# Scaling a chunk's sums of exponentials on ScalarE instead of VectorE, in an attention and maxout feed-forward kernel

## The chip, the core and the metric

The kernel runs on one core of a Trainium2 chip. The metric is device time of one execution in microseconds (us). The core has TensorE (PE, with its weight loads PEld), VectorE (DVE), ScalarE (ACT), GpSimd (POOL) and SyncE (SP), which issues DMAs. Each engine has a queue of its own, works it off in order, and waits on semaphores for the others.

## The reference: what is computed

Attention over 8 batches and 12 heads, 448 rows of 64, with normalised queries and keys, and a feed-forward layer with the larger of three products:

```python
q_n, k_n = rmsnorm(q, g_q), rmsnorm(k, g_k)
scores = np.matmul(q_n, k_n.transpose(0, 1, 3, 2)) / np.sqrt(64)
scores = scores - np.max(scores, axis=-1, keepdims=True)
attn = np.exp(scores)
attn = attn / (np.sum(attn, axis=-1, keepdims=True) + 1e-09)
x = np.matmul(attn, v)        # heads side by side: 3584 x 768
h = np.maximum(np.maximum(x @ w1, x @ w2), x @ w3)
out = h @ w_out
```

All tensors are float32. The weights are 768x768.

## The kernel before, in words

**Tiling.** Two heads make a pair; there are 48 pairs, six for each batch. A pair's 448 query rows are cut into four chunks of 112 rows. One chunk's scores, 112 rows by 448 keys for each of the two heads, lie in one PSUM tile `sc`, of which there are two (`bufs=2`). So the scores of chunk k+1 can't be written before chunk k-1 has been read for the last time.

**Two kinds of pairs.** The first six pairs (`PLAIN = 6`) work in float32. From the seventh pair on, each float32 value is split into an upper and a lower float16 part, and a product takes three matmuls. The change touches only this second kind: 42 pairs, 168 chunks.

**One chunk from the seventh pair on.** `scores` (L553) writes `sc` on PE. `row_max` (L562, DVE) takes the negative maximum of each row. `softmax` runs on ACT: L570 scales the maxima into `nm`, and L579 takes the exponentials of each head in place, with the sums of a row accumulated into two spare columns of `sc`; the trace shows each as an ACTIVATE and a short read of the accumulator. `upper_weights` makes the factor of a row: add the epsilon, scale by 2^-15, invert (`rs`, L648 and L652, both DVE). Then ACT multiplies the exponentials by it and keeps the upper half as float16 (`pp`, L655, one for each head). `lower_weights` (L665, DVE) makes the lower half, and with it the last read of `sc`. `turn_weights` transposes `pp` by DMA, and a pair later `add_values` (L703, PE) multiplies by the values.

**What runs beside it.** The next pair's keys and queries are split on ACT (`kp`, `qp`, L434) and POOL (L440), their squares are summed on DVE (L372). The feed-forward layer of the batch before is spread over the chunks: PE does 18 matmuls for each block of the hidden layer (L732), ACT copies the first product (`m`, L742), DVE takes the maxima (L746), ACT and DVE split the result (`ht`, L752 and L756), and the second product leaves through ACT (`osb`, L805). A pair's attention output is split by ACT (`xt`, L717) and DVE (L718). Until about 285 us the weights are still being decoded and split, on DVE and ACT as well.

**What sets the order.** The program is written out by hand. A pair has 12 beats, three to a chunk. In the first beat of a chunk stand its row maximum, its softmax and the lower half of the chunk before; in the second `upper_weights`; in the third the scores of the next chunk. Each beat ends with a share of the feed-forward matmuls and with work that was put off by a number of beats (`later`). What a beat issues lands in the engines' queues in that order, so between an engine's part of `softmax` and of `upper_weights` stands whatever else the first beat gave to it.

Of the kernel before, what the change touches and what calls it, by code (L numbers as in the profile page):

```python
# [12 lines left out]
AF = mybir.ActivationFunctionType  # L13
ALU = mybir.AluOpType
# [4 lines left out]
SUM_EPS = 1e-9  # L19
# [7 lines left out]
P_UP = 2.0 ** 15  # L27
# [12 lines left out]
def qknorm_attention_maxout_ffn_kernel(  # L40
# [35 lines left out]
    nc = tc.nc  # L76
    B, H, S, D = q.shape
# [4 lines left out]
    QP = S // NQ  # L82
# [561 lines left out]
    def upper_weights(g, c):  # L644
        s = st[g]
        sc = s["sc", c]
        rs = sb.tile([QP, 2], F32, name="rs", bufs=3)
        nc.vector.tensor_scalar(  # L648
            out=rs, in0=sc[:QP, 1, S + 8:S + 10], scalar1=SUM_EPS, scalar2=1.0 / P_UP,
            op0=ALU.add, op1=ALU.mult,  # L650
        )
        nc.vector.reciprocal(rs, rs)  # L652
        pp = sb.tile([QP, 2, 2, S], F16, name="pp", bufs=3)
        for h in range(2):
            nc.scalar.activation(  # L655
                pp[:, 0, h], sc[:QP, h, :S], AF.Copy, scale=rs[:, h:h + 1]
            )
        s["pp", c] = pp
        s["rs", c] = rs
# [196 lines left out]
    for i, src in enumerate((g_q, g_k)):  # L856
        nc.scalar.dma_start(
            out=gains[:, i], in_=src.rearrange("(o d) -> o d", o=1).broadcast_to([P, D])
# [61 lines left out]
    def beat(g, i):  # L920
# [15 lines left out]
        if part == 1:  # L936
            if 0 < k <= 4 * PLAIN:
                keep_turned(*divmod(k - 1, 4))
            if PLAIN <= g < G:
                upper_weights(g, c)  # L940
# [123 lines left out]
```

## Time and profile before

| | |
|---|---|
| runs, us | 1097.57, 1104.33, 1100.64 (median 1100.64) |
| the profiled execution | 1099.43 us, span 1097.6 us |
| instructions in the profile | 18387 |
| mean granted PE clock | 0.964 |

The span is the time from the first to the last instruction of the program. A row of the timeline has the start and the length in us, then engine, line, operation, tiles and shapes; behind `x1` may stand the idle time before it and what ended it. A row of the waits has the waiting engine, tile and line, what it waited for, the total in us, the number of waits and the longest. A row of a group has the number of instructions, their busy time in us, the mean of one in ns, then the engine's idle time ahead of them.

### The profile page before, as it was taken

Reading aid. Unit: us, or ns where it says so; the run is one execution under the profiler, and the core shown is the slowest. Engines: PE = TensorE matmul, PEld = TensorE weight load, DVE = VectorE, ACT = ScalarE, POOL = GpSimd, SP = SyncE. Lnnn points to the kernel's source line nnn. Section 1 sums busy time; section 2 is a strip of 40 time slices with the busy share of each in tenths; the row PEclk is TensorE's granted clock in tenths of the full one; section 3 lists DMA queues with packets and bytes.
Section 4 is the critical chain, followed back from the end, with each engine's and each line's share of the span. In section 5 each row is a group of like instructions: output and inputs, shape, how many; then the busy total and the mean of one; then the engine's idle time right before and its main releaser. Section 6 shows DMA issues by size and latency. Waiting matters only on the chain. (4 is left out here: it accounts for less than half of the span.)

```text
span 1097.6 us, 18387 instructions
## 1 busy us (share of the span) xinstructions
PE 1011.4 (92%) x6168; PEld 499.4 (45%) x6168; DVE 755.7 (69%) x1390; ACT 771.8 (70%) x1767; POOL 704.2 (64%) x805
## 2 busy tenths in 40 slices
PE   4678769888899999999999999999999999999998
PEld 2333334334444454444544454444444554445554
DVE  4799988888767676777677767777676766761110
ACT  4598888767878687787877787777777787863101
POOL 5477988866767777677777776777777677610000
PEclk9697869999999999999999999999999999999999
DMA  5554566855887779778887798787877797553002
GB/s 152 164 168 149 131 183 135 192 116 121 164 156 143 145 153 179 152 148 144 168 156 147 138 168 172 148 145 155 174 145 140 140 178 142 108 100 73 1 1 57
DMA packets 426493, 152.28 MB, mean 139 GB/s; under 512 B 372896, under 2 KB 422048, under 8 KB 426400
## 3 DMA queue, kind: packets, MB, share of 16 engines
q1 hardware_dynamic: 425888, 150.95, 67.7%
q8 instruction: 48, 0.79, 0.3%
q14 instruction: 45, 0.37, 0.1%
q10 hardware_dynamic: 512, 0.18, 0.1%
HBM read 51.97 MB, written 11.01 MB: 57 GB/s over the span
## 5 line engine op out<-in xcount | busy, mean ns | idle before, releaser
L732 PE MATMUL acc<-xt,w_sb 128*128 128x448 f16 x2592 | 516.8, 355 | 0.0
L732 PEld LDWEIGHTS <-w_sb 128*128 128x128 f16 x2592 | 244.1, 98 | 259.3 <-issue 47.9
L579 ACT ACTIVATE sc<-sc,nm,down 112x448 f32<-112x448 f32 x336 | 234.2, 697 | 11.2
L562 DVE TENSOR_REDUCE sc<-sc 112x2 f32<-112x896 f32 x192 | 209.6, 1092 | 46.0 <-PE sc L553 44.7
L655 ACT ACTIVATE pp<-sc,rs 112x448 f16<-112x448 f32 x336 | 194.8, 632 | 46.6 <-ACT sc L579 40.9
L665 DVE SCALAR_TENSOR_TENSOR pp<-sc,rs,pp 112x448 f16<-112x448 f32 x336 | 212.9, 675 | 3.4 <-ACT pp L655 2.9
L387 POOL TENSOR_TENSOR ri<-ri,half_neg 128x7 f32<-128x7 f32 x96 | 154.2, 1606 | 8.0
L553 PE MATMUL sc<-kt,qt 64*112 64x448 f16 x1008 | 131.9, 367 | 28.8 <-DVE pp L665 25.0
L570 ACT ACTIVATE nm<-sc,down 112x2 f32<-112x2 f32 x192 | 50.7, 264 | 147.5 <-DVE sc L562 146.1
L796 PE MATMUL acc<-wo_sb,ht 128*128 128x384 f16 x864 | 151.0, 329 | 1.5 <-DVE ht L756 0.8
L761 POOL COPY hx<-ht 128x128 f16<-128x128 f16 x48 | 15.5, 323 | 197.1 <-DVE ht L756 191.1
L796 PEld LDWEIGHTS <-ht 128*128 128x128 f16 x864 | 81.6, 99 | 67.2 <-issue 13.5
L703 PE MATMUL av<-pt,vp 128*64 128x448 f16 x1008 | 108.3, 356 | 0.0
L553 PEld LDWEIGHTS <-qt 64*112 64x112 f16 x1008 | 54.8, 126 | 98.3 <-issue 57.8
L648 DVE TENSOR_SCALAR rs<-sc 112x2 f32<-112x2 f32 x168 | 26.6, 158 | 94.6 <-ACT sc L579 94.6
L440 POOL TENSOR_TENSOR kp<-kn,kp 128x512 f16<-128x512 f32 x42 | 50.0, 1191 | 58.9 <-ACT kp L434 58.9
L703 PEld LDWEIGHTS <-vp 128*64 128x64 f16 x1008 | 49.6, 108 | 55.7 <-issue 30.0
L718 DVE SCALAR_TENSOR_TENSOR xt<-av,xt 128x448 f16<-128x448 f32 x42 | 26.2, 625 | 70.8 <-ACT xt L717 70.8
L372 DVE TENSOR_REDUCE ss<-sq 128x7 f32<-128x448 f32 x96 | 60.9, 635 | 10.6 <-ACT sq L363 6.6
L531 POOL TENSOR_TENSOR vp<-vr,vp 128x448 f16<-128x448 f32 x42 | 43.8, 1044 | 30.3 <-ACT vp L525 30.2
L440 POOL TENSOR_TENSOR qp<-qn,qp 112x512 f16<-112x512 f32 x42 | 49.2, 1173 | 19.8 <-ACT qp L434 19.8
L517 POOL TENSOR_SCALAR vr<-vr,v_up 128x448 f32<-128x448 f32 x42 | 61.1, 1456 | 0.0
(112 smaller groups left out, 1200.4 us busy)
## 6 DMA issues: line engine op xcount, KB each, us to landing
raw<-in_moe_w_dram SPq DMA_DIRECT2D x18, 768.0 KB, 4.5
qr<-in_q_dram SPq DMA_DIRECT2D x48, 224.0 KB, 3.1
vr<-in_v_dram SPq DMA_DIRECT2D x96, 96.0 KB, 2.6
kr<-in_k_dram SPq DMA_DIRECT2D x95, 96.0 KB, 3.1
raw<-in_moe_w_out_dram SPq DMA_DIRECT2D x6, 768.0 KB, 5.0
pt<-pp SPq DMA_TRANSPOSE x168, 4.0
out_dram<-osb SPq DMA_DIRECT2D x8, 336.0 KB, 3.2
out_dram<-osb SPq DMA_DIRECT2D x8, 288.0 KB, 3.6
```

What stands on the lines that cost most here:

```text
L372: nc.vector.tensor_reduce(sums[g % 2][:sq.shape[0], KQ[what]], sq, axis=AX, op=ALU.add)
L387: nc.gpsimd.tensor_tensor(out=ri, in0=ri, in1=half_neg[:, at], op=ALU.pow)
L440: nc.gpsimd.tensor_tensor(out=parts[:, 1], in0=n, in1=parts[:, 0], op=ALU.subtract)
L517: nc.gpsimd.tensor_scalar(out=vr, in0=vr, scalar1=v_up[:, g // NP:g // NP + 1], scalar2=None, op0=ALU.mult,)
L553: nc.tensor.matmul(sc[:QP, h, :S], qt[rows, qp, c], kt[rows, kp, KEYS[h]], start=n == 0, stop=n == len(TERMS) - 1,)
L562: nc.vector.tensor_reduce(sc[:QP, 0, S + 8:S + 10], sc[:QP, :, :S], axis=AX, op=ALU.max, negate=True)
L579: nc.scalar.activation(to, sc[:QP, h, :S], AF.Exp, bias=nm[:, h:h + 1], scale=down[:QP], accum_out=total,)
L655: nc.scalar.activation(pp[:, 0, h], sc[:QP, h, :S], AF.Copy, scale=rs[:, h:h + 1])
L665: nc.vector.scalar_tensor_tensor(out=pp[:, 1, h], in0=sc[:QP, h, :S], scalar=rs[:, h:h + 1], in1=pp[:, 0, h], op0=ALU.mult, op1=ALU.subtract,)
L703: nc.tensor.matmul(av[half, :S], vp[rows, group, vpart], pt[rows, 7 * wp + group], start=u == 0 and n == 0, stop=u == 3 and n == len(TERMS ...
L732: nc.tensor.matmul(acc[:, :S], wt[:, wp, c], xs[c][:, xp], start=(c == 0 and n == 0), stop=(c == NCT - 1 and n == 2),)
L796: nc.tensor.matmul(acc[:, :HW], lhs, wo_sb[:, f, wp, half * HW:(half + 1) * HW], start=(f == 0 and n == 0), stop=(f == NFT - 1 and n == 2),)
```

## The change

In `upper_weights` the epsilon is added and the scaling done by an ACTIVATE (Copy) with constant bias and scale on ScalarE, so sums·2^-15 + epsilon·2^-15; VectorE only inverts.

```diff
         rs = sb.tile([QP, 2], F32, name="rs", bufs=3)
-        nc.vector.tensor_scalar(
-            out=rs, in0=sc[:QP, 1, S + 8:S + 10], scalar1=SUM_EPS, scalar2=1.0 / P_UP,
-            op0=ALU.add, op1=ALU.mult,
+        nc.scalar.activation(
+            rs, sc[:QP, 1, S + 8:S + 10], AF.Copy, bias=SUM_EPS / P_UP, scale=1.0 / P_UP
         )
         nc.vector.reciprocal(rs, rs)
```

All lines behind it move up by one (L655 becomes L654, and so on).

ScalarE's queue in the first chunk of a pair, with the split of the next pair's keys (`kp`) and a copy of the feed-forward layer (`m`) between the exponentials and `pp`; before:

```order
L570 ACTIVATE nm<-sc,down 112x2 [waits DVE_49]
L579 ACTIVATE sc<-sc,nm,down 112x448 [waits Activation_49] x2
L434 CAST kp<-kn_90 128x512 [waits DMAHW2_49]
L742 COPY m<-acc 128x448
L655 ACTIVATE pp<-sc,rs 112x448 [waits DMAHW1_49,DVE_49,Activation_49]
L655 ACTIVATE pp<-sc,rs 112x448
L434 CAST qp<-qn 112x512 [waits DMAHW3_49]
```

and with the change:

```order
L570 ACTIVATE nm<-sc,down 112x2 [waits DVE_49]
L579 ACTIVATE sc<-sc,nm,down 112x448 [waits Activation_49] x2
L434 CAST kp<-kn_90 128x512 [waits DMAHW2_49]
L741 COPY m<-acc 128x448
L648 ACTIVATE rs<-sc 112x2 [waits Activation_49]
L654 ACTIVATE pp<-sc,rs 112x448 [waits DMAHW1_49,DVE_49]
L654 ACTIVATE pp<-sc,rs 112x448
L434 CAST qp<-qn 112x512 [waits DMAHW3_49]
```

The scaling stands behind both pieces and right ahead of `pp`.

VectorE's queue from the lower half of the chunk before to the next row maximum, in the same chunk; before:

```order
L665 SCALAR_TENSOR_TENSOR pp<-sc,rs,pp 112x448
L648 TENSOR_SCALAR rs<-sc 112x2 [waits Activation_49]
L652 RECIPROCAL rs<-rs 112x2 [waits DVE_49]
L372 TENSOR_REDUCE ss_87<-sq 128x7 [waits Pool_49]
L746 TENSOR_TENSOR m<-acc,m 128x448 [waits PE_49,Activation_49]
L562 TENSOR_REDUCE sc<-sc 112x2 [waits PE_49]
```

and with the change:

```order
L664 SCALAR_TENSOR_TENSOR pp<-sc,rs,pp 112x448
L651 RECIPROCAL rs<-rs 112x2 [waits Activation_49]
L372 TENSOR_REDUCE ss_87<-sq 128x7 [waits Pool_49]
L745 TENSOR_TENSOR m<-acc,m 128x448 [waits PE_49]
L562 TENSOR_REDUCE sc<-sc 112x2 [waits DVE_49,PE_49]
```

The reciprocal now waits for ScalarE itself, everything behind it stands as before, and the row maximum names VectorE's own semaphore too.

## The prediction

> **What bounds the kernel now.** I read the page's busy shares first, then busy time by stretches, then the waits of two stretches, then single chunks in the timeline.
>
> ```profile
> PE 1011.4 (92%) x6168; PEld 499.4 (45%) x6168; DVE 755.7 (69%) x1390; ACT 771.8 (70%) x1767; POOL 704.2 (64%) x805
> ```
>
> TensorE (PE) is busy 92% of the span, VectorE (DVE) and ScalarE (ACT) 70%. The chain of work that ended last lies in the last 108 us, where no chunk is left, and tells nothing of the part that is changed. The stretches do:
>
> ```profile
> 145.00:285.00 140.00, 117.53 (x696) 55.97 (x692) 118.98 (x209) 107.93 (x233) 109.16 (x110) 0.94 0.70 145
> 450.00:900.00 450.00, 445.40 (x2829) 217.22 (x2828) 323.49 (x639) 343.88 (x807) 325.43 (x391) 1.00 0.81 154
> ```
>
> The columns are PE, PEld, DVE, ACT, POOL, then clock and DMA. From 145 to 285 us (pairs seven to twelve, while weights are still being decoded) PE idles 22 of 140 us and DVE is busy 85%. From 450 to 900 PE idles only 4.6 of 450 us. Who waits for whom in these two zones, first 140 to 287, then 287 to 992:
>
> ```profile
> PE sc L553 <- DVE pp L665: 18.2, 10, 3.9
> DVE sc L562 <- PE sc L553: 1.7, 2, 1.2
> ...
> DVE sc L562 <- PE sc L553: 43.0, 34, 2.2
> ACT pp L655 <- ACT sc L579: 38.5, 74, 0.7
> ACT pp L655 <- DVE rs L652: 2.1, 3, 0.7
> PE sc L553 <- DVE pp L665: 6.8, 14, 1.3
> ```
>
> In the first zone PE waits for DVE's lower_weights (L665), which frees the score buffer that the next scores (L553) fill: the loop of DVE and ACT is the bound, with 1.7 us of slack in it. In the second zone it is the other way round: DVE waits 43.0 us for scores before its row maximum (L562), and PE waits 6.8 us. That 43.0 us is the loop's whole reserve there.
>
> The loop of one chunk is: row maximum on DVE, nm and two exponentials on ACT, sums and reciprocal on DVE, what DVE has queued, the next row maximum. Three chunks of it, the last row of each exponential first:
>
> ```profile
> 602.51 0.13 ACT L579 ACTIVATION_READ_ACCUMULATOR sc<-sc,nm,down 112x1 f32 x1
> 602.56 0.62 ACT L434 CAST kp<-kn 128x512 f16<-128x512 f32 x1
> 602.87 0.17 DVE L652 RECIPROCAL rs<-rs 112x2 f32<-112x2 f32 x1
> 603.12 1.16 ACT L655 ACTIVATE pp<-sc,rs 112x448 f16<-112x448 f32 x2
> ...
> 613.03 0.13 ACT L579 ACTIVATION_READ_ACCUMULATOR sc<-sc,nm,down 112x1 f32 x1
> 613.20 0.16 DVE L648 TENSOR_SCALAR rs<-sc 112x2 f32<-112x2 f32 x1 [0.73 <-ACT sc L579]
> 613.39 0.17 DVE L652 RECIPROCAL rs<-rs 112x2 f32<-112x2 f32 x1
> 613.64 1.16 ACT L655 ACTIVATE pp<-sc,rs 112x448 f16<-112x448 f32 x2 [0.48 <-ACT sc L579]
> ...
> 617.37 0.13 ACT L579 ACTIVATION_READ_ACCUMULATOR sc<-sc,nm,down 112x1 f32 x1
> 617.78 0.15 DVE L648 TENSOR_SCALAR rs<-sc 112x2 f32<-112x2 f32 x1
> 617.96 0.17 DVE L652 RECIPROCAL rs<-rs 112x2 f32<-112x2 f32 x1
> ...
> 624.10 0.17 DVE L652 RECIPROCAL rs<-rs 112x2 f32<-112x2 f32 x1
> 624.30 0.54 ACT L742 COPY m<-acc 128x448 f32<-128x448 f32 x1
> 624.72 1.18 ACT L655 ACTIVATE pp<-sc,rs 112x448 f16<-112x448 f32 x2
> ```
>
> In a **bare** chunk (613) ACT has nothing between its exponentials and pp and stands still 0.48 us for DVE. In a **covered** chunk (602, 624) ACT does one or two other pieces there, and DVE finishes the reciprocal beside them, at no cost. ACT's waits count the bare ones in the second zone: 74 + 3 = 77 of its 144 chunks; the other 67 are covered.
>
> **The change part by part.** Prices first:
>
> ```profile
> L570 ACT ACTIVATE nm<-sc,down 112x2 f32<-112x2 f32 x192 | 50.7, 264 | 147.5 <-DVE sc L562 146.1
> L619 ACT ACTIVATE sum<-sum 112x8 f32<-112x8 f32 x6 | 1.4, 235 | 0.0
> L652 DVE RECIPROCAL rs<-rs 112x2 f32<-112x2 f32 x168 | 27.9, 166 | 5.8
> L648 DVE TENSOR_SCALAR rs<-sc 112x2 f32<-112x2 f32 x168 | 26.6, 158 | 94.6 <-ACT sc L579 94.6
> L665 DVEq EVENT_SEMAPHORE  x163: 21/50/195, 162.6 to 992.2; - x163
> ```
>
> Removed: 168 DVE operations of 158 ns, 26.6 us of DVE time. Added: 168 ACT operations on the same 112x2 sums. No row has exactly this form. Nearest are nm (264 ns, same shape from PSUM, but the scale read from a tile) and the guard of the first six pairs (235 ns, Copy with constants, 8 elements from SBUF). I take 235, since constants are the nearer form, and keep 264 above; below it I let it be as quick as DVE's 158. That is 39.5 us more ACT time, 811 of 1098 us: as a share, no bound.
>
> In a sentence apart: the Trainium skill (ScalarE: Activation LUTs, What ACT_TABLE_LOAD costs) gives an ACTIVATE with constants 186 ns plus 0.833 ns an element, and 93 ns more for each operand read from a tile, so an estimate of 188 ns here; the trace's 235 for 8 elements is above its 193, and by the page's price the sum below would come out some 7 us lower.
>
> What costs is the place. The new operation stands in ACT's queue behind the covering pieces, right ahead of pp, and the reciprocal must wait for it; hand-overs are read from the rows: 0.04 us from ACT to DVE, 0.08 from DVE's end to pp.
> - Bare: exponential ends 613.16, reciprocal ended 613.56. Now 613.18 + 0.235 + 0.04 + 0.166 = 613.62: +0.06 us.
> - One covering piece: ACT is free at 603.12. Reciprocal ends 603.12 + 0.235 + 0.04 + 0.166 = 603.56 instead of 603.04: +0.52. And pp starts 0.08 later, 603.64 instead of 603.12: ACT too loses 0.52.
> - Two pieces: 624.72 + 0.44 = 625.16 instead of 624.27: +0.89; three are worse.
> - Late DVE (617): DVE comes to the sums 0.28 us after the exponentials' end; the reciprocal can now take the place of the sums' scaling: 0.16 to 0.18 earlier, a gain.
>
> Queued behind the waiting reciprocal on DVE are the sum of squares (L372), the feed-forward's maximum and lower part (L746, L756), the next row maximum and lower_weights, for which PE's scores wait. Behind the waiting pp on ACT are the q cast, ht, m and xt, of which ht and xt hold DVE up in turn. No DMA is moved; the transposes behind pp and kp follow their producers. One more thing in the instruction order: of 192 row maxima 133 now wait for an earlier DVE operation besides PE. That one ended a chunk before, so I price only the extra wait: 0.02 us, between 0 and the median of 0.05 that lower_weights' own separate wait takes (last row above, min/median/max in ns).
>
> Sum, zone one (24 chunks, 7 bare): 10 with one piece, 4 with two, 3 with three, counted in the timeline. The pieces here are longer:
>
> ```profile
> 162.06 0.17 DVE L652 RECIPROCAL rs<-rs 112x2 f32<-112x2 f32 x1
> 163.92 1.15 ACT L655 ACTIVATE pp<-sc,rs 112x448 f16<-112x448 f32 x2
> ```
>
> This reciprocal goes from 162.23 to 163.92 + 0.44 = 164.36, +2.1. Chunk by chunk the 24 give 13 us of delay. Slack is 1.7, so **+11**; at worst 13, at best 0 if DVE's decode fills its new waits.
>
> Sum, zone two: 77 bare, of which some 27 with late DVE, give about −1 together; 50 singly covered at 0.5 give 25; 17 with more at 1.0 give 17. In all 41 us of delay against 43.0 us of reserve. It would just fit, were both spread alike. They are not. Take the twelve pairs from 599.7 to 840, a pattern that recurs:
>
> ```profile
> DVE sc L562 <- PE sc L553: 13.5, 11, 2.2
> ...
> 608.12 0.77 PE L553 MATMUL sc<-kt,qt 64*112 64x448 f16 x6 [1.26 <-DVE pp L665]
> 614.53 1.10 DVE L562 TENSOR_REDUCE sc<-sc 112x2 f32<-112x896 f32 x1 [0.97 <-PE sc L553]
> ...
> 829.73 1.10 DVE L562 TENSOR_REDUCE sc<-sc 112x2 f32<-112x896 f32 x1 [1.48 <-PE sc L553]
> ```
>
> The reserve sits once in a pair, before its last row maximum, and is (first and last of the 11 rows above) 0.97, 0, 2.13, 2.19, 0.98, 0.25, 1.47, 0.69, 1.52, 1.61, 0.25 and 1.48 us. The delays, worked out the same way, are 0.5, 1.54, 2.05, 0.5, 0.95, 1.48, 0.88, 0.95, 2.5, 0.5, 1.93 and 0.88. Where the delay is larger the excess stays: 1.54 + 1.23 + 0.26 + 0.98 + 1.68 = 5.7 us in 240. Over the zone's 705 us that is 17. The extra wait adds about 2. **+19**; at best 0 (the two-deep score buffer carries the excess into the next pair's reserve), at worst 41 (PE's own delay moves the reserve along, so none of it is used).
>
> Together 11 + 19 = 30. The profiled execution took 1099.43 us (span 1097.6), which becomes 1129.4; the median of the runs, 1100.64, lies 1.2 above it, which would make 1130.6. I say **1130**.
>
> **The rivals.**
> - *Reserve fully used.* Zone two costs nothing, zone one 11: 1111 to 1112. For it: delay and reserve are equal in sum. Against it: one pair in four has 0.25 us of reserve or none, and there the delay is about 1.5 or more.
> - *Reserve not used at all.* 13 + 41 = 54: 1155. For it: PE already stands 1.26 us for lower_weights at 608.12, and where it does, any delay of the loop is PE's too. Against it: most pairs show DVE waiting for PE a full microsecond.
> - *Hidden.* DVE's decode in zone one does not depend on the reciprocal and fills the new waits: 1101 to 1105. Against it: each engine's queue is in order, and the decode stands behind the reciprocal.
> - *Faster.* DVE bounds zone one, and gets back 0.19 us (613.20 to 613.39) in each chunk: 24 chunks, 4.6 us; over all 168 chunks 32 us, 1069 at the most. It decides where ACT has the sums scaled before DVE comes to the reciprocal, as in the chunk at 617. Against it: DVE waited 94.6 us for ACT's exponentials before the 168 scalings, so it is ACT that is late there, and ACT gets the work.
>
> **How the numbers follow.** The forecast has 0.68, reserve not used 0.14, reserve used 0.10, hidden 0.04, faster 0.04. A change of 1% is 11 us, about what a measurement of this kernel can tell from no change; between 1090 and 1112 lie the hidden case and parts of the one with the reserve used and of the faster one: 0.10. Slower by more: 0.88; faster by more: 0.02. The range takes in zone one alone (1111) and most of the way to no reserve (1155): 1110 to 1152.
>
> **What would show it.** Right: ACT has 168 operations of about 0.235 us at L648; DVE's waits ahead of the reciprocal grow from 94.6 us to some 160 to 180 (0.28 more in a bare chunk, 0.7 or more in a covered one); DVE's wait for scores in the second zone falls well under 43 us; PE's wait for lower_weights grows there from 6.8 us by some 15; bare chunks pass almost unchanged. Wrong: PE's idle time in 450 to 900 stays at 5 us (then the reserve held), or zone one is no longer than before (then the decode fills the waits), or the reciprocal comes sooner in covered chunks (then the order on ACT isn't what I take it for).

## The result and the profile after

Six runs each: the medians are 1110.53 us with the change (1108.65 to 1111.37) and 1098.34 before (1097.57 to 1104.33). The ratio, taken over all runs and not from the two medians, is 1.0097, 95% interval 1.0078 to 1.0116: about 10.7 us slower. The direction is the forecast one; the size, +30, is nearly three times too large. The profiled execution took 1108.65 us, its span is 1106.9.

The page's busy shares with the change:

```profile
PE 1014.5 (92%) x6168; PEld 497.3 (45%) x6168; DVE 722.1 (65%) x1222; ACT 796.6 (72%) x1935; POOL 705.0 (64%) x805
```

VectorE's busy time fell by 33.6 us, and ScalarE's rose by 24.8. Neither share says anything of the time. The new operation itself (minimum, median and maximum in ns), and the matmuls of the scores, which are as long as before:

```profile
L648 ACT ACTIVATE rs<-sc x168: 152/173/202, 147.1 to 998.9; 112x2 f32<-112x2 f32 x168
L553 PE MATMUL sc<-kt,qt x1008: 346/349/620, 135.9 to 995.5; 64*112 64x448 f16 x168
```

The operation takes 173 ns, not 235. The waits from 290 us on, where before 43.0 us stood for VectorE's wait for scores and 6.8 us for PE's wait for lower_weights:

```profile
DVE rs L651 <- ACT rs L648: 142.9, 126, 2.3
...
ACT pp L654 <- DVE rs L651: 33.6, 143, 0.3
DVE sc L562 <- PE sc L553: 29.2, 28, 2.0
PE sc L553 <- DVE pp L664: 11.5, 17, 1.4
```

VectorE's reserve before its row maxima fell from 43.0 to 29.2 us, and PE waits 4.7 us longer for lower_weights. From 450 to 900 us PE now idles 450 − 442.26 = 7.7 us, before 4.6. So the mechanism is there, weaker than reckoned.

Three kinds of chunk with the change, 7 to 8.5 us later in the run than the same chunks before it: covered by the keys' split, bare, and covered by ht:

```profile
609.75 0.14 ACT L579 ACTIVATION_READ_ACCUMULATOR sc<-sc,nm,down 112x1 f32 x1
609.80 0.62 ACT L434 CAST kp<-kn 128x512 f16<-128x512 f32 x1
610.31 0.18 ACT L648 ACTIVATE rs<-sc 112x2 f32<-112x2 f32 x1
610.53 0.17 DVE L651 RECIPROCAL rs<-rs 112x2 f32<-112x2 f32 x1 [0.80 <-ACT rs L648]
610.73 1.16 ACT L654 ACTIVATE pp<-sc,rs 112x448 f16<-112x448 f32 x2 [0.23 <-DVE rs L651]
...
620.64 0.14 ACT L579 ACTIVATION_READ_ACCUMULATOR sc<-sc,nm,down 112x1 f32 x1
620.81 0.17 ACT L648 ACTIVATE rs<-sc 112x2 f32<-112x2 f32 x1
621.01 0.17 DVE L651 RECIPROCAL rs<-rs 112x2 f32<-112x2 f32 x1 [0.94 <-ACT rs L648]
621.22 1.16 ACT L654 ACTIVATE pp<-sc,rs 112x448 f16<-112x448 f32 x2 [0.23 <-DVE rs L651]
...
641.79 0.17 DVE L651 RECIPROCAL rs<-rs 112x2 f32<-112x2 f32 x1 [1.26 <-ACT rs L648]
641.87 0.60 DVE L755 SCALAR_TENSOR_TENSOR ht<-acc,ht 128x448 f16<-128x448 f32 x1
642.39 1.09 DVE L562 TENSOR_REDUCE sc<-sc 112x2 f32<-112x896 f32 x1
```

From the exponentials' end to the reciprocal's end a covered chunk now takes 610.70 − 609.89 = 0.81 us, before 603.04 − 602.64 = 0.40: +0.41, where +0.52 was forecast. The scaling starts at 610.31, 0.11 before the cast's end, and pp 0.03 after the reciprocal's end, not 0.08. The bare chunk takes 621.18 − 620.78 = 0.40: unchanged.

### The profile page after: what moved, and what is told of

Same layout as the page of the kernel before. It is cut to its first block, busy times and chain, and to the rows that moved or that the text cites. A ratio compares the mean times of both kernels' runs of the same rounds, so it can differ in the third digit from the quotient of the medians.

```text
span 1106.9 us, 18554 instructions
## 1 busy us (share of the span) xinstructions
PE 1014.5 (92%) x6168; PEld 497.3 (45%) x6168; DVE 722.1 (65%) x1222; ACT 796.6 (72%) x1935; POOL 705.0 (64%) x805
## 4 chain that ended last, share of the span: by engine, by line
PE 51%; ACT 19%; DVE 18%; issue 6%; DMA 2%; POOL 1%; SPq 1%; DVEq 0%; ACTq 0%; POOLq 0%
PE acc L731 23%; PE acc L795 10%; PE av L702 8%; PE sc L553 7%; ACT sc L579 6%; DVE sc L562 6%; DVE pp L664 4%; ACT pp L654 3%; ACT e L579 2%; PE av L691 1%; ACT nm L570 1%; ACT xt L716 1%; DMA pt<-pp 1%; DVE v_rows L170 1%; DVE m L745 1%
## 5 line engine op out<-in xcount | busy, mean ns | idle before, releaser
L579 ACT ACTIVATE sc<-sc,nm,down 112x448 f32<-112x448 f32 x336 | 234.2, 697 | 11.2
L654 ACT ACTIVATE pp<-sc,rs 112x448 f16<-112x448 f32 x336 | 194.5, 630 | 41.9 <-DVE rs L651 40.5
L553 PE MATMUL sc<-kt,qt 64*112 64x448 f16 x1008 | 132.5, 369 | 33.5 <-DVE pp L664 29.5
L651 DVE RECIPROCAL rs<-rs 112x2 f32<-112x2 f32 x168 | 27.7, 165 | 169.2 <-ACT rs L648 168.9
L553 PEld LDWEIGHTS <-qt 64*112 64x112 f16 x1008 | 53.2, 127 | 105.5 <-issue 46.4
```

The costliest lines, as they stand in the source:

```text
L553: nc.tensor.matmul(sc[:QP, h, :S], qt[rows, qp, c], kt[rows, kp, KEYS[h]], start=n == 0, stop=n == len(TERMS) - 1,)
L579: nc.scalar.activation(to, sc[:QP, h, :S], AF.Exp, bias=nm[:, h:h + 1], scale=down[:QP], accum_out=total,)
L654: nc.scalar.activation(pp[:, 0, h], sc[:QP, h, :S], AF.Copy, scale=rs[:, h:h + 1])
```

## The experiments

The chip's own difference between runs comes first, since it sets what a trace can tell. The first scores of the seventh pair are issued ahead of everything that the change touches, and yet they start anywhere from 135.3 to 138.4 us after the span's start in these profiles. So traces are compared by stretches: zone one from those scores to the first ones of the thirteenth pair, zone two from there to the last chunk's. The starts of these three groups of L553 in the timelines give the stretches; before, they are 136.55, 284.51 and 985.84 us. Times are medians over all runs of one call, the ratios are taken over all these runs, with their 95% intervals.

The stretches come from one execution each, so small differences between them are not read. In zone two, where PE is the bound, its busy time for the same matmuls was 691.1 us before and 689.4 in e9, so that some 2 us there say nothing of the loop. In zone one the granted clock was 0.92 before and 0.89 with the change, but that is not what made it longer: at 0.90 e9 and e11 took 147.6 and 147.7 us there, no more than before.

| kernel | median us, with that of the kernel before in the same call | ratio | zone one, us | zone two, us |
|---|---|---|---|---|
| before | | | 148.0 | 701.3 |
| the change | 1110.53, 1098.34 | 1.0097 (1.0078 to 1.0116) | 153.0 | 706.2 |
| e1: scaling early on ScalarE | 1100.33, 1099.73 | 1.0009 (1.0000 to 1.0019) | 149.9 | 700.1 |
| e2: first chunks alone | 1108.83, 1099.73 | 1.0087 (1.0073 to 1.0100) | 149.2 | 709.0 |
| e3: other chunks alone | 1100.97, 1099.73 | 1.0008 (0.9999 to 1.0018) | 151.5 | 697.5 |
| e4: unused scaling | 1097.96, 1099.73 | 0.9985 (0.9976 to 0.9994) | 147.5 | 700.7 |
| e8: three unused | 1100.30, 1099.45 | 1.0008 (0.9995 to 1.0020) | 148.7 | 701.6 |
| e10: change, squares ahead | 1101.71, 1099.45 | 1.0022 (1.0013 to 1.0031) | 150.7 | 701.0 |
| e11: before, squares ahead | 1096.61, 1099.45 | 0.9973 (0.9962 to 0.9984) | 147.7 | 700.8 |
| e9: last chunks alone, from pair 13 on | 1096.02, 1099.45 | 0.9965 (0.9952 to 0.9977) | 147.6 | 696.8 |
| e12: late pp | 1101.02, 1100.30 | 1.0016 (1.0004 to 1.0028) | 147.7 | 703.0 |
| e6: scaling in two steps | 1129.63, 1100.30 | 1.0273 (1.0259 to 1.0287) | 156.5 | 721.1 |
| e7: no scaling | 1093.42, 1100.30 | 0.9942 (0.9929 to 0.9954) | 145.5 | 696.2 |
| e13: e9 and e11 together | 1094.87, 1100.30 | 0.9953 (0.9939 to 0.9966) | 146.7 | 698.8 |

The theory after the result was that the place of the scaling in ScalarE's queue costs the time (P), against the work or the hand-over as such (W).

**e1: the scaling right behind the exponentials.**

```diff
                 softmax(g, c)
+                if g >= PLAIN:
+                    scale_sums(g, c)      # the ScalarE scaling of the change
```

> ScalarE scales the sums right behind its two exponentials, ahead of the covering pieces; VectorE's reciprocal stays where it is. Theory P (place): what the change costs is that the scaling stands behind the covering pieces, so that the reciprocal comes 0.41 us later in a covered chunk. Moved ahead of them it delays the reciprocal by about 0.02 us in every chunk and the covering pieces by 0.17: the time is that of the kernel before, within -2 to +4 us. Rival W (work): 168 more ScalarE operations and one more hand-over in each chunk cost the time wherever they stand: +8 to +12 us, as in the change.

Measured: +0.1%, at most +0.2%: 1 us. The ScalarE work and the hand-over are the same as in the change, and nearly all of the 10.7 us is gone. W falls.

**e2 and e3: the change in a pair's first chunk, or in the other three.**

```diff
+        if c == 0:      # e3: c > 0
+            nc.scalar.activation(
+                rs, sc[:QP, 1, S + 8:S + 10], AF.Copy, bias=SUM_EPS / P_UP, scale=1.0 / P_UP
+            )
+        else:
             nc.vector.tensor_scalar(
```

> The change in the first chunk of each pair alone (42 of 168, all of them covered by the split of the next keys). Theory P: the reciprocal comes 0.41 to 0.85 us later in just these chunks, and part of it is taken up by VectorE's wait for scores later in the pair: +5 to +8 us of the change's 10.7. Rival W: a quarter of the operations, a quarter of the cost: +2.7 us. If the reserve before a pair's last row maximum takes up what it can, this part and the one with the other three chunks add up to less than the change.

> The change in the second, third and fourth chunk of each pair alone (126 of 168, of which 84 are bare and 42 covered). Theory P: 84 bare chunks cost 0.01 us each, the late ones gain 0.2, and only the covered ones are delayed: +1 to +4 us. Rival W: three quarters of the operations, three quarters of the cost: +8 us.

Measured: a quarter of the operations cost 0.87%, 9.6 us, more than expected; three quarters cost 0.08%. PE's waits for lower_weights from 290 us on, first e2, then e3:

```profile
PE sc L553 <- DVE pp L670: 14.9, 20, 1.6
```

```profile
PE sc L553 <- DVE pp L670: 4.8, 5, 1.4
```

In zone two the first chunks lose 7.7 us, the others gain 3.8; in zone one they lose 1.2 and 3.5. The parts add up (3.9 of 4.9, and 4.7 of 5.0; by the runs 0.95% of 0.97%). The expectation that the two parts would together come to less than the whole, because reserve takes up some of each, did not show.

**e4 and e8: unused ScalarE work at that place.** Ahead of pp stand scalings whose result nobody reads, one in every chunk (e4) or three in a pair's first chunk (e8); VectorE's scaling and reciprocal as before.

```diff
         nc.vector.reciprocal(rs, rs)
+        if c == 0:                       # e8; e4: one, in every chunk, ahead of the reciprocal
+            for n in range(3):
+                nc.scalar.activation(spare, sc[:QP, 1, S + 8:S + 10], AF.Copy, ...)
```

> The kernel before, with one more ScalarE operation of the change's form on the same sums and at the same place, whose result nobody reads. The reciprocal waits for VectorE alone, as before; only ScalarE's time goes up by 168 x 0.17 = 29 us. Theory P: in a bare chunk ScalarE stands 0.48 us idle there and nothing moves; in a covered one pp starts 0.12 to 0.17 later and the reciprocal does not: 0 to +3 us. Rival W, in its form that ScalarE's work is what costs: +8 to +12 us.

> The kernel before, with three unused ScalarE scalings ahead of pp in the first chunk of each pair, whose results nobody reads: pp and all behind it on ScalarE come 0.35 to 0.45 us later there, about as late as in the change (0.36), while VectorE's scaling and reciprocal stay as early as before. The change in the first chunk alone cost 9 us. Theory D (VectorE's queue): that cost comes from the reciprocal that holds up VectorE's queue and with it the next row maximum, so here it is 0 to +3 us. Rival A (ScalarE's queue): it comes from the later pp, so here it is +6 to +10 us.

Measured: e4 0.15% faster, outside what was expected; its profile is 0.5 and 0.6 us shorter in the two zones, and why an unused operation should shorten them stays open. What was asked, whether more ScalarE work costs 8 to 12 us, is answered: no. e8 +0.08%. But e8 did not test what it was built for, as its ScalarE timeline shows:

```profile
603.49 0.62 ACT L434 CAST kp<-kn 128x512 f16<-128x512 f32 x1
604.00 0.30 ACT L656 ACTIVATE spare<-sc 112x2 f32<-112x2 f32 x3
604.16 0.66 ACT L662 ACTIVATE pp<-sc,rs 112x448 f16<-112x448 f32 x1
```

Three such operations that don't wait for each other take 0.30 us together, and pp starts 0.16 after the first of them, not 0.35 to 0.45. So e8 decides nothing between the two queues; e12 does it with one longer operation.

**e12: pp alone later.**

```diff
         nc.vector.reciprocal(rs, rs)
+        if c == 0:
+            spare = sb.tile([QP, 360], F16, name="spare", bufs=1)
+            nc.scalar.copy(spare, sc[:QP, 0, :360])      # nobody reads it
```

> The kernel before, with one unused ScalarE cast of 112x360 ahead of pp in the first chunk of each pair, whose result nobody reads. Three unused small scalings made pp only 0.16 us later; this one is sized from the 0.54 us of a 112x448 copy to make it 0.3 to 0.4 later, as in the change's first chunk (0.39), while the reciprocal stays as early as before. Theory D (VectorE's queue): 0 to +3 us. Rival A (ScalarE's queue): +6 to +10 us, what the change in the first chunk alone costs.

Averaged over the first chunks of zone two (the start of pp against the end of L579), pp came 0.32 us later, in the change 0.39, and the reciprocal did not move. Measured: +0.16%, 1.8 us, where e2 lost 9.6. The later pp is the small part.

**e10 and e11: the sum of squares ahead.** It goes into the wait before the first chunk's reciprocal, in the change (e10) and in the kernel before (e11).

```diff
             if PLAIN <= g < G:
+                if i == 1 and n < G:
+                    sum_squares(n, "k")
                 upper_weights(g, c)
...
-            if i in (2, 5):
+            if i == 5 or i == 2 and g < PLAIN:
                 sum_squares(n, "kq"[i // 3])
```

> The change, but from the seventh pair on the sum of squares of the keys after next (0.60 us on VectorE, its input ready over 2 us before) stands ahead of the first chunk's reciprocal in VectorE's queue instead of behind it, and runs while VectorE waits there for ScalarE (0.80 us in the pair at 607). Theory D: the next row maximum then comes 0.5 us earlier than in the change, which is what that chunk lost: 0 to +4 us over the kernel before. Rival A: pp is as late as in the change, so the cost stays at +9 to +11 us.

> The kernel before with the same move: the sum of squares ahead of VectorE's scaling and reciprocal in a pair's first chunk. VectorE waits 0.2 to 0.74 us for the exponentials there, and the 0.60 us go into that wait; the reciprocal comes up to 0.4 us later, but ScalarE is busy with the keys' split until 0.08 us after the old reciprocal's end and may stand 0.3 us. Theory D: the next row maximum comes up to 0.5 us earlier in each pair, -2 to -6 us, less than the 9 us that 0.41 us of delay cost, since the loop has reserve in two pairs of three. Rival A: no gain, 0 to +4 us from the later pp.

In e10 the first chunk around 604 us looks like this:

```profile
604.33 0.61 DVE L372 TENSOR_REDUCE ss<-sq 128x7 f32<-128x448 f32 x1
604.45 0.13 ACT L579 ACTIVATION_READ_ACCUMULATOR sc<-sc,nm,down 112x1 f32 x1
...
605.00 0.18 ACT L648 ACTIVATE rs<-sc 112x2 f32<-112x2 f32 x1
...
605.22 0.17 DVE L651 RECIPROCAL rs<-rs 112x2 f32<-112x2 f32 x1 [0.29 <-ACT rs L648]
605.42 1.16 ACT L654 ACTIVATE pp<-sc,rs 112x448 f16<-112x448 f32 x2 [0.23 <-DVE rs L651]
```

VectorE's wait is 0.29 instead of 0.80 us; reciprocal and pp are as late as in the change, and only what is queued behind them on VectorE comes earlier. That brings +0.97% down to +0.22%. Theory D's forecast is met and rival A's is not: the first chunks' loss runs through VectorE's queue. But the move is worth something without the change too. It makes the kernel before 0.27% faster by its runs (its profiled execution was the slowest of the eleven and shows only 0.8 us of that in the two zones). So with the squares ahead in both kernels the change still costs 1.0022 / 0.9973, or 0.49%: the move takes away about half of the change's own cost, not three quarters. In the profiles what is left lies in zone one (150.7 against 147.7 us; zone two has 701.0 against 700.8), where the longest covers stand in third chunks, which the move doesn't touch.

**e9: last chunks alone, from the thirteenth pair on.** The condition of e2 with `c == 3 and g >= 2 * NP`.

> The change in the last chunk of a pair alone, and only from the thirteenth pair on (36 chunks), where no weights are decoded. In the run with the change in the other three chunks the trace gains 3.8 us in that stretch. Theory D: the gain comes from the last chunks, where VectorE comes to the sums late, so that ScalarE has them scaled before and the reciprocal comes 0.2 us earlier: -2 to -4 us. Rival: it comes from the second and third chunks, or from what lies beside; then 0 within 1 us.

Measured: −0.35%, and in zone two −4.5 us, no less than the 3.8 that e3 gained there; some 1.7 of the 4.5 is PE's shorter busy time (691.1 and 689.4 us). Its last chunk of the pair at 600 us:

```profile
616.14 0.13 ACT L579 ACTIVATION_READ_ACCUMULATOR sc<-sc,nm,down 112x1 f32 x1
616.31 0.17 ACT L649 ACTIVATE rs<-sc 112x2 f32<-112x2 f32 x1
616.55 0.15 DVE L657 RECIPROCAL rs<-rs 112x2 f32<-112x2 f32 x1
616.74 1.16 ACT L660 ACTIVATE pp<-sc,rs 112x448 f16<-112x448 f32 x2 [0.26 <-DVE rs L657]
```

VectorE comes late (the chunk at 617 before the change), finds the sums scaled, and does not wait: the reciprocal ends 616.70 − 616.27 = 0.43 us behind the exponentials, before 618.13 − 617.50 = 0.63. But not every last chunk is late. Of the 35 that another pair follows, 17 gain such a 0.20 us, 11 are covered and lose about 0.35, and 7 are bare and stay. At the next row maximum that is 4.2 us gained and 3.3 lost, nearly even. What makes it a gain in time is, as far as the traces tell, where each falls. Before the change the late ones stand ahead of pairs with 0.62 us of reserve on average (8 of the 17 with 0.25 or none), the covered ones ahead of pairs with 1.76. No run separates the two kinds.

**e6: the scaling in two dependent steps.** This makes the delay at least as long as the prediction took it to be, to test its arithmetic of the reserve alone.

```diff
-        nc.scalar.activation(rs, sc[:QP, 1, S + 8:S + 10], AF.Copy, ...)
+        nc.scalar.activation(first, sc[:QP, 1, S + 8:S + 10], AF.Copy, ...)
+        nc.scalar.activation(rs, first, AF.Copy, bias=0.0, scale=1.0)
```

> The change with the scaling in two ScalarE steps, the second waiting for the first, so that reciprocal and pp come some 0.2 us later than in the change in every chunk, bare ones too. The loop then grows by about 0.48 + 4 x 0.2 = 1.3 us a pair from 290 to 990 us, about what the prediction took for the change. Theory E (the excess of each pair over its own reserve is lost, as the prediction reckoned): 14 us there, 10 before, +22 to +28 us over the kernel before. Rival C (what one pair lacks the next pair's reserve makes good, so that only the growth above the whole reserve of 43 us is lost): +10 to +14 us.

The second step's length in ns, and the waits from 290 to 1000 us:

```profile
L652 ACT ACTIVATE rs<-first x168: 203/203/205, 148.8 to 1019.3; 112x2 f32<-112x2 f32 x168
```

```profile
PE sc L553 <- DVE pp L666: 25.4, 30, 1.7
DVE sc L562 <- PE sc L553: 10.8, 24, 0.7
```

Measured: +2.73% (2.59 to 2.87), 30 us. To the end of zone two, here at 1015 us, VectorE's wait for scores is 12.0 us. So the reserve used is 43.0 − 12.0 = 31.0 us, the time lost in zone two 721.1 − 701.3 = 19.8; together 51 us in 36 pairs, 1.4 a pair. The time lies above E's range of 22 to 28 us, and far above C's of 10 to 14: C falls.

**e7 and e13: what could be gained.** e7 leaves out epsilon and scaling (the reciprocal reads `sc`, and `finish` scales by 1.0), e13 joins e9 and e11.

> Neither engine scales: VectorE inverts the sums straight away. Left out are the epsilon, and the factor 2^15 in the weights with its inverse behind the values. Against the kernel before, the reciprocal comes 0.19 us earlier in bare chunks, in covered ones ScalarE's pp stays where it is. Theory D (the loop runs through the reciprocal on VectorE's queue): the loop is 0.19 us shorter in each chunk, mostly into the reserve from 290 us on and into time before that: -3 to -8 us. Rival: PE is the bound, 0 to -2 us.

> The two gains together: the kernel before, with the sum of squares ahead of the first chunk's scaling, and ScalarE's scaling in the last chunk of a pair alone from the thirteenth pair on. Alone they brought -2.9 and -3.4 us. Theory D: both shorten the same loop, so that together they bring less than the sum: -4 to -6 us. Rival: each takes the other's reserve: no more than -3.5.

Measured: −0.58% and −0.47%. In e7 VectorE's wait for scores from 290 us on shows where most of the shorter loop goes:

```profile
DVE sc L562 <- PE sc L553: 56.5, 49, 2.6
```

The reserve grew by 13.5 us, the time of zone two fell by 5.1. e13 is faster than the kernel before and the changed one and computes what they compute; it brings 5.2 us by its ratio. That is less than the sum of its two parts (6.8), as theory D has it, but within their intervals, so the difference is not shown.

## Why the prediction was right in direction and wrong in size

- **The bound and the mechanism: right.** The loop through the row maximum, ScalarE and the reciprocal decides before 285 us, and has a reserve after. e1 puts the cost on the place of the scaling, e10 to e12 put that of the first chunks on VectorE's queue behind the waiting reciprocal. The forecast also gave the late chunks a gain of 0.16 to 0.18 us each; in e9 it is 0.20. VectorE's waits ahead of the reciprocal grew from 94.6 to 168.9 us, inside the 160 to 180 foretold:

```profile
L651 DVE RECIPROCAL rs<-rs 112x2 f32<-112x2 f32 x168 | 27.7, 165 | 169.2 <-ACT rs L648 168.9
```

- **The price of the operation: too high.** "I take 235, since constants are the nearer form": it takes 173 ns, inside the bounds of 158 and 264. Both ScalarE rows lie too high. nm has the same shape and source, but its scale is read from a tile. The guard reads SBUF and eight elements: e6's second step, with constants and two elements from SBUF, takes 203, so that the source explains 30 ns of the 62, and the rest stays open. The Trainium skill's price (ScalarE: Activation LUTs, What ACT_TABLE_LOAD costs), an estimate of 188 ns, was the nearer one.
- **The failed step: "The delays, worked out the same way, are 0.5, 1.54, 2.05 …", in all 41 us in zone two.** Measured the growth of the loop is 13.8 us of reserve used plus 4.9 us of time, 18.7. Two errors are in it. The first is each delay's size. Summed over zone two the reciprocals come 31 us later behind their exponentials: 23.2 in first chunks, where 19 with one piece and 17 with more made 27 in the reckoning, and 7.7 in the others, where it had 15. The price is lower, and ScalarE starts the scaling 0.11 us before the cast ends. The second error, about as large, takes the 31 down to 18.7: I let the reciprocal's delay pass in full to the next row maximum. Take the pair from 620.91, for which I reckoned 1.54. VectorE's rows before the change are the row maxima of its first and second chunks, then from its third chunk, and last the next pair's row maximum:

```profile
620.91 1.09 DVE L562 TENSOR_REDUCE sc<-sc 112x2 f32<-112x896 f32 x1
625.42 1.09 DVE L562 TENSOR_REDUCE sc<-sc 112x2 f32<-112x896 f32 x1
...
633.44 0.17 DVE L652 RECIPROCAL rs<-rs 112x2 f32<-112x2 f32 x1
633.71 0.62 DVE L756 SCALAR_TENSOR_TENSOR ht<-acc,ht 128x448 f16<-128x448 f32 x1
634.31 1.10 DVE L562 TENSOR_REDUCE sc<-sc 112x2 f32<-112x896 f32 x1
...
639.93 1.09 DVE L562 TENSOR_REDUCE sc<-sc 112x2 f32<-112x896 f32 x1
```

  Before, ht stood 0.10 us from the reciprocal's end and waited for ScalarE; with the change (641.87 above) it starts 0.09 ahead of that end, and the row maximum 0.52 behind ht's start instead of 0.60. Of the 0.33 us by which this reciprocal is late, nearly all is taken up; the row maximum comes 0.05 later. Over the whole pair the row maxima move apart by 0.67 us (639.93 − 620.91 = 19.02 before; 647.96 − 628.27 = 19.69 with the change), nearly all of it, 0.66, in the first chunk (633.44 − 628.27 = 5.17; before 625.42 − 620.91 = 4.51):

```profile
628.27 1.09 DVE L562 TENSOR_REDUCE sc<-sc 112x2 f32<-112x896 f32 x1
633.44 1.09 DVE L562 TENSOR_REDUCE sc<-sc 112x2 f32<-112x896 f32 x1
...
647.96 1.09 DVE L562 TENSOR_REDUCE sc<-sc 112x2 f32<-112x896 f32 x1
```

  Averaged over zone two, the way from a chunk's row maximum to the next grew by 0.47 us in first chunks, where the reciprocals come 0.65 later, and by nothing in second and last ones; the third ones' end at the wait for PE, where the reserve is. The 2 us for the extra wait of the row maxima were not seen: in 25 second chunks that are bare the next row maximum comes within 0.01 us of where it came before.
- **The reserve, pair by pair: right as a rule.** e6 used 31 of the 43 us and still lost 19.8; the change used 13.8 and lost 4.9. The twelve reserves of the prediction, each set against the mean growth of a pair, leave an excess of 5.3 us at e6's 1.4 a pair, and of 1.1 at the change's 0.52: over 36 pairs 16 and 3, by 4 and 2 us too little, since the growth is not the same in every pair. The loss goes faster than the delay, so that a growth 2.2 times too large (41 for 18.7) became a time 4 times too large (19 for 4.9). That e6 lost 19.8, near the forecast 19, is chance: its growth was 51 us, not 41.
- **Zone one: 11 foretold, 5.0 measured.** Here the sizes were nearly right and the same second step failed. In the prediction's example the reciprocal ended 162.23 − 161.80 = 0.43 us behind the exponentials before, and now 163.44 − 160.96 = 2.48, so 2.1 later, as reckoned. The ends of the exponentials, before and with the change:

```profile
161.67 0.13 ACT L579 ACTIVATION_READ_ACCUMULATOR sc<-sc,nm,down 112x1 f32 x1
```

```profile
160.82 0.14 ACT L579 ACTIVATION_READ_ACCUMULATOR sc<-sc,nm,down 112x1 f32 x1
...
163.27 0.17 DVE L651 RECIPROCAL rs<-rs 112x2 f32<-112x2 f32 x1 [2.15 <-ACT rs L648]
```

  Over the 24 chunks the reciprocals come 12.1 us later, where 13 was reckoned, but the next row maxima only 6.5. The two longest covers pass their 4 us on nearly in full; in the other chunks what stands behind the reciprocal takes up most of the delay.
- **The rivals.** "Reserve fully used", at 1111 to 1112, came out at the measured time, but not for its reason: it had 11 in zone one and nothing in zone two, and each gave 5. "Not used at all" is excluded by 29.2 us of reserve left, "hidden" and "faster" by the interval.
- **The range.** It began at 1110, and the runs' median lies just inside. That is luck: the low end stood for 11 us in zone one and none in zone two, and what came was 5 in each. The chance of 0.88 for slower by over 1% was too sure for a growth whose two factors were both read off single chunks.

## What to carry to other kernels

What the moved operation cost here was what it then stood behind in the other engine's queue, not its own length: ask what is ahead of it there, and what is queued behind whoever waits. Follow a delay through to the next step that closes the loop, row by row, before multiplying it; waits and overlaps on the way take much of it. And where the reserve is spread unevenly, reckon the loss pair by pair, since it grows faster than the delay; the same edit can gain in a part of the loop where the waiting engine comes late anyway (17 of the 35 last chunks in e9) and lose elsewhere.

## What the runs showed of the hardware that I had not expected

A 112x2 ScalarE operation with constants takes 173 ns from PSUM and 203 ns from SBUF (medians of 168 each), against 262 (median of 192) from PSUM with the scale read from a tile. Three of them that are independent take 0.30 us together, so that beside other work one of them takes an estimated 0.06 us of the queue, (0.30 − 0.18) / 2; in e4, 168 of them that nobody waited for cost no time. And a VectorE operation behind a reciprocal of 0.17 us can start 0.08 us after that one's start.
